# Float16 parts of q and k from the second pair of heads on, in an attention, Fourier and FFN kernel on one core

## The chip, the cores and the metric

The kernel runs on one core of a Trainium2 chip. The metric is the device time of one execution in microseconds. The kernel before took 1229.35 us, the median of three runs (1228.66 to 1231.81).

The engines are named as the profile names them: PE is TensorE, PEld its weight load, DVE is VectorE, ACT is ScalarE, POOL is GpSimd, SP is SyncE, which only issues DMAs.

## The reference

```python
def _attn_ref(q, k, v):                      # q, k, v: (8, 8, 576, 64) float32
    scores = scale * np.matmul(q, k.transpose(0, 1, 3, 2))
    scores = np.where(block_i >= block_j, scores, -1000000000.0)   # blocks of 64
    scores = scores - np.max(scores, axis=-1, keepdims=True)
    attn = np.exp(scores)
    attn = attn / (np.sum(attn, axis=-1, keepdims=True) + 1e-09)
    return np.matmul(attn, v)

def _moe_ref(x, w_ch1, w_ch2):               # x: (8, 576, 512), heads joined
    X = np.fft.fft(np.fft.fft(x, axis=1), axis=2)
    u = x + np.real(X)
    un = (u - mean(u)) / np.sqrt(var(u) + 1e-06)
    return u + np.maximum(un @ w_ch1, 0.0) @ w_ch2      # 512 -> 2048 -> 512
```

## The kernel before, in words

There are 8 batches of 8 heads. For each batch the kernel computes attention head by head, writes the result x to a DRAM tile (`xd`), reads it back straight and mirrored by rows, does a two-stage real Fourier transform by matmuls, normalizes, and sends the result through the two FFN matrices. All the matmuls work at close to float32 precision: an operand is split into a high and a low float16 part (or a float32r tile is used), and the products of the parts are summed in PSUM.

**A head.** `lead` and `rest` tiles hold q and k of a head side by side. `max_part` (L576) multiplies the high parts of q and k in four groups of matmuls, DVE reduces each to the row maxima `M`; `shift` (L605) transposes `M` on PE, ACT writes it as the row `mt`, and a DMA of 1.2 KB puts that row into the `lead` tile, so that the scores come out shifted. `scores` (L635) is four pieces: matmuls of `rest` and `lead`, then ACT makes the exponential twice (`ph` in float16, `p` in float32) and POOL subtracts them to the low part `pl`. `values` (L663) multiplies `ph` and `pl` by the parts of v (`VH`, `VL`) into `av`; after the last chunk DVE divides (`DEN`, `rec`, and `x` or `zc`), and after each second head two DMAs write to `xd`.

**How q and k get there.** Heads 0 to 7, the first batch, go by float32: `load_head` (L367) loads one head (64 rows of 1152 values, 295 KB), `lead` (L420) copies it on ACT into the tile of type float32r, `rest` (L430) takes the remainder of q on DVE and of k on POOL, and `lead_copies` puts two DMAs of 147 KB beside it. From head 8 on, pairs of heads go by float16: `load_pair` (L373) loads 128 rows (590 KB), `sum_qk` (L379) squares q and k on ACT for their sums, `scale` (L460) adds the sums over the partitions with one matmul and makes a power of two on DVE, `high` writes the scaled float16 parts on ACT, `low` the differences on DVE, and `high_copies` (L403) and `low_copies` (L413) bring each head's parts by two and two DMAs from the pair's tiles into the head's (147 KB and 295 KB). Three tiles `lead` and `rest` (`NB = 3`) are shared in turn by the heads.

**The weights.** Meanwhile the FFN's weights are loaded in 18 pieces by ACT's queue, brought from 64-bit integers' words to single precision by DVE (`W<-W`, three operations for a piece), and split: `weight_high` on ACT and `weight_parts` on PE and ACT for the first matrix.

**What sets the order.** All of this is written as lanes of `Step` objects. A planner in the same function keeps a clock of its own and books each step's chain on the engines' queues (D is DVE, A is ACT, G or P is POOL, Q is SP, M the DMA engines); `ready` (L298) says when a step may start, `issue` (L314) books and emits it, and the loop at L1248 chooses the next step by readiness and by `place`, a number near the head's. Steps with a cost use PE; steps of cost 0 ("free" steps) only use other engines and DMAs. The FFN's steps are the filler: one is issued whenever no step of a lane is ready. Each engine then runs its instructions in the order in which they were emitted. While the filler has not begun, all seven PSUM banks are lent to the other steps (`lent`).

**The transform.** `mirror` (L749) loads the first 256 rows (`u`) and 33 more (`X`) of `xd` on SP's queue, and gathers the mirrored rows by three indirect DMAs on POOL's. `folded` (L769) adds or subtracts straight and mirrored rows on DVE, in the order chunk 2 (33 rows), 0, 1.

Of the kernel before, what the change touches and what calls it, by code (L numbers as in the profile page):

```python
# [22 lines left out]
P = 128  # L23
# [8 lines left out]


HOP = 0.25
MARGIN = 0.3
AHEAD = (3.0, 6.0)
FREE = 0.5

# [163 lines left out]
def tile_attn_fourier_ffn(  # L202
# [47 lines left out]
    LEAD = [work.tile([P, 64 + 2 * S], F32R, name=f"lead{i}", bufs=1) for i in range(NB)]  # L250
    REST = [work.tile([P, 2 * S], F32R, name=f"rest{i}", bufs=1) for i in range(NB)]
    X1, X0, QA, QB = [], [], [], []

    def half_tiles():

        for i in range(NB):
            a = work.tile([P, 64 + 2 * S], F32, name=f"lead{i}", bufs=1).bitcast(F16)
            b = work.tile([P, 2 * S], F32, name=f"rest{i}", bufs=1).bitcast(F16)
            X1.append(a[0:KS, 0:64 + 2 * S])
            QA.append(a[:, 64 + 2 * S:64 + 4 * S])  # L260
            X0.append(b[:, 0:2 * S])
            QB.append(b[:, 2 * S:])
# [6 lines left out]
    for i in range(NB):  # L269
        gpsimd.dma_start(LEAD[i][D:KS], c_masks)  # L270
        vector.tensor_scalar(LEAD[i][0:D, 0:64], ones[0:D, 0:64], 0.0, None, op0=ALU.mult)
# [26 lines left out]
    def ready(step):  # L298
        r = max((done[x] for x in step.after), default=0.0)
        return max(r, min(rings[x][0] for x in lent)) if step.bank else r  # L300

    def book(engine, t, cost):

        used = [queues[x] for x in {"X": "DK", "G": "GK", "P": "G"}.get(engine, engine)]
        while True:
            at = max(x.fit(t, cost) for x in used)
            if at <= t:
                return max(x.book(t, cost) for x in used)
            t = at
# [63 lines left out]
    def load_pair(g):  # L373

        raws["pair", g] = work.tile([P, 2 * S], F32, name="raw", bufs=2)
        sync.dma_start(raws["pair", g], qk[2 * g:2 * g + 2].rearrange("h d s -> (h d) s"))
        yield

    def sum_qk(g):  # L379
        if not X1:  # L380
            half_tiles()
        raw, acc = raws["pair", g], sums(g)
        scalar.activation(QA[g % 2][:, 0:S], raw[:, 0:S], AF.Square, accum_out=acc[:, 1:2])
        yield
        scalar.activation(QB[g % 2][:, S:], raw[:, S:], AF.Square, accum_out=acc[:, 2:3])
        yield

    def high(g):
        raw, sc = raws["pair", g], scales[g]
        scalar.activation(QA[g % 2][:, 0:S], raw[:, 0:S], AF.Copy, scale=sc[:, 1:2])  # L390
        yield
        scalar.activation(QB[g % 2][:, S:], raw[:, S:], AF.Copy, scale=sc[:, 2:3])
        yield

    def low(g):
        raw, sc = raws.pop(("pair", g)), scales[g]
        a, b = QA[g % 2], QB[g % 2]
        vector.scalar_tensor_tensor(b[:, 0:S], raw[:, 0:S], sc[:, 1:2], a[:, 0:S], op0=ALU.mult, op1=ALU.subtract)
        yield
        vector.scalar_tensor_tensor(a[:, S:], raw[:, S:], sc[:, 2:3], b[:, S:], op0=ALU.mult, op1=ALU.subtract)  # L400
        yield

    def high_copies(h):  # L403
        x, at = X1[h % NB], slice(D * (h % 2), D * (h % 2 + 1))
        if h < H + NB:
            sync.dma_start(x[D:KS], c_masks16)
            vector.memset(x[0:D, 0:64], 0.0)
        g = h // 2
        sync.dma_start(x[0:D, 64:64 + S], QA[g % 2][at, 0:S])
        sync.dma_start(x[0:D, 64 + S:], QB[g % 2][at, S:])  # L410
        yield

    def low_copies(h):  # L413
        x, at = X0[h % NB], slice(D * (h % 2), D * (h % 2 + 1))
        g = h // 2
        sync.dma_start(x[0:D], QB[g % 2][at])
        sync.dma_start(x[D:P], QA[g % 2][at])
        yield
# [41 lines left out]
    def scale(g):  # L460

        acc = vsums.pop(g)
        t = ps_tile()
        mm(t[:, 0:3], ones, acc[:, 0:3], start=True, stop=True)
# [3 lines left out]
        vector.tensor_copy(n2, t[:, 0:3])  # L468
# [4 lines left out]
        for i in (1, 2):  # L473
# [3 lines left out]
        vector.tensor_scalar(  # L477
            x[:, 0:1], bits[:, 0:1], 0x7F000000, 1, op0=ALU.bitwise_and, op1=ALU.logical_shift_right
        )
        vector.tensor_scalar(to[:, 0:1], x[:, 0:1], -1, (190 + 14) << 23, op0=ALU.mult, op1=ALU.add)  # L480
# [14 lines left out]
    def split_v(g):  # L495

        acc = vsums.pop(g)
# [4 lines left out]
        sc = acc[:, 2:3]  # L502
        x = work.tile([P, 1], I32, name="pw", bufs=2)
        vector.tensor_copy(acc[:, 1:2], t[:, 0:1])
        vector.tensor_scalar(
            x, acc[:, 1:2].bitcast(I32), 0x7F000000, 1, op0=ALU.bitwise_and, op1=ALU.logical_shift_right
# [10 lines left out]
    def head_lane():  # L517
        for h in range(H):
            yield Step(
                lambda: load_head(h), 0.0, ("Q0.6", "M1.0", "L2.0"), (("T2", h - 2, 0), ("T2", h - 2, 1)) if h > 1 else (), ("L", h), place=h - 2.2  # L520
            )

        for g in range(H // 2, B * H // 2):
            done_with = (("T2", g + 2, 0), ("T2", g + 2, 1)) if g < H // 2 + 2 else (("lo", g - 2),)
            yield Step(lambda: load_pair(g), 0.0, ("Q0.6", "M2.2", "L2.0"), done_with, ("L", g), place=2 * g - 3.4)

    def pair_lane():
        for g in range(H // 2, B * H // 2):
            yield Step(
                lambda: sum_qk(g), 0.0, ("A0.86", "A0.86"), (("L", g),), ("QS", g), place=2 * g - 1.8,  # L530
# [818 lines left out]
```

## Time and profile before

| | us |
|---|---|
| median of three runs | 1229.35 |
| the profiled execution | 1229.43 |
| its span, first to last instruction | 1227.2 |
| PE busy in the span | 1146.5 (93%) |
| DVE busy | 693.3 (56%) |
| ACT busy | 564.2 (46%) |
| POOL busy | 423.2 (34%) |

Busy time is what an engine spends executing; waiting, branching and DMA-issuing are not in it. The granted clock (PEclk) is the share of PE's full clock that the chip let through. The chain of waits goes back from the last instruction to whatever released it, step by step, so a DMA stands in it with the time from its issue to the instruction that used it. Instructions of nearly all engines are recorded by one helper line (L195; L217 for matmuls), so groups are told apart by the names of the tiles that they write and read.

### The profile page before, as it was taken

The numbers are of one execution on the slowest core, as the hardware profiler recorded it, in microseconds if no ns is written. First come the engines' busy times: TensorE is split into PE (matmuls) and PEld (weight loads), VectorE is DVE, ScalarE is ACT, GpSimd is POOL, SyncE is SP. The second block draws the span as 40 slices with busy tenths as digits, with TensorE's granted clock in tenths as the row PEclk, the third lists the DMA queues.
The fourth block names the chain that finished last, engine by engine and source line by source line (L and its number), as shares of the span: only waits on it lengthen the run. The fifth ranks groups of instructions, "written<-read, shape, count | busy, mean of one in ns | idle before, by whom it ended". The sixth has DMA issues, their size and how long they took to land.

```text
span 1227.2 us, 25303 instructions
## 1 busy us (share of the span) xinstructions
PE 1146.5 (93%) x10116; PEld 823.7 (67%) x10116; DVE 693.3 (56%) x1514; ACT 564.2 (46%) x1257; POOL 423.2 (34%) x514
## 2 busy tenths in 40 slices
PE   5766878999899999999999999999999999999998
PEld 4663556576677777677777777776777667666665
DVE  6876777657747674766557555766474325431211
ACT  5565749655455445545465455644543112111110
POOL 4652525444333434354242633462425101200000
PEclk9566989999899999999999999999999999999999
DMA  7685344433224232421453224414230110000000
GB/s 208 176 296 177 108 129 113 113 109 87 73 71 126 74 87 70 135 65 47 117 150 82 80 65 130 108 38 124 60 96 15 37 37 6 18 18 1 18 18 18
DMA packets 65099, 107.38 MB, mean 87 GB/s; under 512 B 9504, under 2 KB 35304, under 8 KB 64982
## 3 DMA queue, kind: packets, MB, share of 16 engines
q1 hardware_dynamic: 57606, 81.37, 23.9%
q10 hardware_dynamic: 4384, 16.78, 4.1%
q0 software_dynamic: 2992, 7.62, 2.4%
q8 instruction: 79, 1.29, 0.5%
q14 instruction: 38, 0.31, 0.1%
HBM read 58.54 MB, written 18.89 MB: 63 GB/s over the span
## 4 chain that ended last, share of the span: by engine, by line
PE 82%; DVE 8%; DMA 3%; POOL 3%; ACT 2%; issue 1%; DVEq 0%; POOLq 0%; ACTq 0%; SPq 0%
PE h L217 30%; PE acc L217 30%; PE ps L217 15%; PE av L217 6%; DVE W L195 2%; DVE M L195 2%; PE ps L220 1%; DMA lead<-mt 1%; POOL pl L195 1%; DMA lead<-rest 1%; POOL u L195 1%; POOL ag L195 1%; DVE tmp L195 0%; DMA lead<-in_c_masks_dram 0%; DMA V<-in_v_dram 0%
## 5 line engine op out<-in xcount | busy, mean ns | idle before, releaser
L217 PE MATMUL h<-uh,W 128*128 128x256 f16 x2304 | 427.9, 273 | 1.2 <-DVE zc L195 1.2
L195 POOL TENSOR_TENSOR pl<-p,ph 128x288 f16<-128x288 f32 (+1 forms) x256 | 259.0, 1024 | 387.8 <-ACT p L195 365.5
L217 PEld LDWEIGHTS <-W 128*128 128x128 f16 x3456 | 332.1, 98 | 62.7 <-issue 2.3
L217 PE MATMUL acc<-W,gh 128*128 128x512 f16 x1104 | 329.6, 380 | 0.0
L217 PE MATMUL h<-ul,W 128*128 128x256 f16 x1152 | 314.4, 273 | 0.0
L195 DVE SCALAR_TENSOR_TENSOR gl<-h,gh 128x512 f16<-128x512 f32 x138 | 94.7, 688 | 208.5 <-ACT gh L195 208.4
L217 PE MATMUL acc<-W,gl 128*128 128x512 f16 x552 | 209.7, 380 | 1.3 <-DVE gl L195 1.3
L195 ACT ACTIVATE gh<-h 128x512 f16<-128x512 f32 x138 | 82.4, 597 | 275.8 <-PE h L217 275.7
L195 DVE TENSOR_REDUCE M<-ps 128x1 fp32r<-128x320 f32 (+3 forms) x293 | 130.9, 482 | 119.4 <-PE ps L217 119.1
L217 PE MATMUL ps<-lead 73*128 73x288 f16 (+13 forms) x702 | 160.8, 292 | 14.6 <-DMA lead<-in_c_masks_dram 7.0
L195 ACT ACTIVATE ph<-ps 128x512 f16<-128x512 f32 (+1 forms) x234 | 118.5, 507 | 111.6 <-PE ps L217 111.0
L217 PEld LDWEIGHTS <-gh 128*128 128x128 f16 x1104 | 102.7, 99 | 84.0 <-issue 3.2
L217 PEld LDWEIGHTS <-ph 128*128 128x128 f16 x1920 | 110.5, 102 | 26.6 <-DVE x L195 3.3
L195 ACT ACTIVATE p<-ps 128x512 f32<-128x512 f32 (+1 forms) x234 | 118.6, 509 | 1.9 <-POOL W L195 0.8
L217 PE MATMUL av<-VH,pl 128*128 128x65 f16 x960 | 113.6, 199 | 5.6 <-POOL pl L195 4.0
L217 PE MATMUL av<-VH,ph 128*128 128x65 f16 x960 | 114.5, 200 | 3.2 <-DVE x L195 1.7
L217 PE MATMUL av<-VL,ph 128*128 128x64 f16 x960 | 113.9, 198 | 0.0
L217 PEld LDWEIGHTS <-gl 128*128 128x128 f16 x552 | 53.8, 97 | 68.4 <-DVE gl L195 3.4
L217 PE MATMUL ps<-rest 128*128 128x320 f16 (+2 forms) x350 | 97.1, 291 | 2.8 <-DVE M L195 2.3
L217 PEld LDWEIGHTS <-pl 128*128 128x128 f16 x960 | 92.5, 101 | 7.0 <-POOL pl L195 5.4
L217 PEld LDWEIGHTS <-lead 73*128 73x128 f16 (+1 forms) x672 | 58.3, 100 | 33.8 <-issue 7.2
L217 PEld LDWEIGHTS <-rest 128*128 128x128 f16 x336 | 33.4, 100 | 22.5 <-issue 3.1
(202 smaller groups left out, 1415.0 us busy)
## 6 DMA issues: line engine op xcount, KB each, us to landing
raw<-in_qk_dram SPq DMA_DIRECT2D x28, 576.0 KB
W<-in_moe_w_ch_dram ACTq DMA_DIRECT2D x14, 1024.0 KB
rest<-lead SPq DMA_DIRECT2D x72, 144.0 KB
V<-in_v_dram SPq DMA_DIRECT2D x32, 320.0 KB
out_dram<-u SPq DMA_DIRECT2D x32, 256.0 KB
rest<-rest SPq DMA_DIRECT2D x56, 144.0 KB
xd<-x SPq DMA_DIRECT2D x30, 256.0 KB
u<-xd SPq DMA_DIRECT2D x8, 512.0 KB
```

Source lines behind the costliest of these rows:

```text
L195: x = f(*args, **kw)
L217: return tc.keep_in_program_order(nc.tensor.matmul(*args, **kw))
L220: return tc.keep_in_program_order(nc.tensor.transpose(*args, **kw))
```

## The change

Only heads 0 and 1 (`HF = 2`) still go by float32. The pair lane now starts at pair 1 (`GF = 1`), so heads 2 to 7 are loaded in pairs, squared, scaled, split and copied as the later batches are. Pair 1 has no tiles free yet: it is loaded as two halves into `zs0` and `zs1` and split into two stage tiles (`stage`, named u), and a weight load into one of those now waits for its copies. For pairs 1 to 3 `scale` makes q's and k's scale alone (`lo = 1`), and the scale of v stays in `split_v`.

Beside that: the 33-row load and the 33-row gather come first in `mirror`; the small tiles for the weights' split are a tile of their own (`turns`) and no longer a buffer of `x`; a free step of a place past 8 is ready only when the engine that it uses first would be open within 3 us of its own time (`BACKLOG`); the planner's hop is 0.3 in place of 0.25; the folds of batch 1 and the first feed's steps carry waits that the planner did not have; and when the filler begins, the planner's clock is set to where the lent PSUM banks are free.

```diff
+HF = 2
+GF = HF // 2
-HOP = 0.25
+HOP = 0.3
+BACKLOG = 3.0
...
     def ready(step):
         r = max((done[x] for x in step.after), default=0.0)
-        return max(r, min(rings[x][0] for x in lent)) if step.bank else r
+        if step.bank:
+            return max(r, min(rings[x][0] for x in lent))
+        if step.place > H and not step.cost:
+            for engine, cost in step.chain:
+                if engine in "DAGXP":
+                    return max(r, opening(engine, max(r, now), cost) - BACKLOG)
+                if engine not in scratch:
+                    break
+        return r
...
     def load_pair(g):
-        raws["pair", g] = work.tile([P, 2 * S], F32, name="raw", bufs=2)
-        sync.dma_start(raws["pair", g], qk[2 * g:2 * g + 2].rearrange("h d s -> (h d) s"))
+        given = qk[2 * g:2 * g + 2].rearrange("h d s -> (h d) s")
+        if g == GF:
+            raws["pair", g] = [work.tile([P, 2 * NSIN], F32, name=f"zs{i}", bufs=1) for i in range(2)]
+            for i in range(2):
+                sync.dma_start(raws["pair", g][i], given[:, S * i:S * (i + 1)])
+        else:
+            t = work.tile([P, 2 * S], F32, name="raw", bufs=2)
+            raws["pair", g] = t[:, 0:S], t[:, S:]
+            sync.dma_start(t, given)
         yield
...
     def pair_lane():
-        for g in range(H // 2, B * H // 2):
+        for g in range(GF, B * H // 2):
             yield Step(
-                lambda: sum_qk(g), 0.0, ("A0.86", "A0.86"), (("L", g),), ("QS", g), place=2 * g - 1.8,
-                need=((("TC", 2 * g - 3),) if g > H // 2 + 1 else (("S", H - 1, 2),)) + (("V", 2 * g - 5, 4),),
+                lambda: sum_qk(g), 0.0, ("A0.86", "A0.86"),
+                (("LP", g),) + ((("TC", 2 * g - 3),) if g > GF + 2 else ()) + ((("V", 2 * g - 5, 4),) if g > 2 else ()),
+                ("QS", g), place=2 * g - 1.8, need=(("S", g % 2, 2),) if GF < g < GF + 3 else (),
             )
+            if g < H // 2:
+                yield Step(lambda: scale(g, 1), 0.11, ("D0.2", "B", "D0.6"), (("QS", g),), ("SC", g), True, place=2 * g - 1.4)
...
     def copy_lane():
-        for h in range(H, B * H):
+        for h in range(HF, B * H):
...
     def prepare_lane():
-        for h in range(H):
+        for h in range(HF):
...
+            sync.dma_start(X[2], xd[256:289])
             sync.dma_start(LL, xd[0:256].rearrange("(c p) d -> p c d", p=P))
-            sync.dma_start(X[2], xd[256:289])
-            for dst, i in ((U[0], 0), (U[1], 1), (U2[0:33], 2)):
+            for dst, i in ((U2[0:33], 2), (U[0], 0), (U[1], 1)):
...
-                both = work.tile([P, 10 * D], F32, name="x", bufs=1)
+                both = work.tile([P, P + P // 2], F32, name="turns", bufs=1)
...
         if i is None:
-            lent = ["ps"]
+            if len(lent) > 1:
+                now = max(now, ready(filler), *rings["h"], *rings["acc"])
+                lent = ["ps"]
```

How the order moves, at three places. First SP's queue at the very start; `lead_84`/`rest_87` belong to head 0, `lead_85`/`rest_88` to head 1, `raw` is a load of q and k. Before:

```order
L195 DMA raw<-in_qk_dram 64x1152
L195 DMA rest_87<-lead_84 64x576 x2
L195 DMA raw<-in_qk_dram 64x1152
L195 DMA rest_88<-lead_85 64x576 x2
L195 DMA lead_84<-mt 1x5x128
L195 DMA V<-in_v_dram 128x640
```

With the change (`zs_124` and `zs_125` take pair 1, `lead_216` and `rest_217` are head 2's, copied from the stage tiles u):

```order
L200 DMA raw<-in_qk_dram 64x1152
L200 DMA zs_124<-in_qk_dram 128x576
L200 DMA zs_125<-in_qk_dram 128x576
L200 DMA rest_86<-lead_84 64x576 x2
L200 DMA raw<-in_qk_dram 128x1152
L200 DMA rest_87<-lead_85 64x576 x2
L200 DMA lead_84<-mt 1x5x128
L200 DMA V<-in_v_dram 128x640
L200 DMA raw<-in_qk_dram 128x1152
L200 DMA lead_85<-mt 1x5x128
L200 DMA lead_216<-in_c_masks_dram 9x1216
L200 DMA lead_216<-u 64x576 x2
```

Two loads of a whole pair now stand in front of head 0's row `mt`, and the copies of heads 2 and 3 follow it.

Second, DVE around the last output of the first batch's last head (`zc<-av,rec`); `VL` is the low part of v of the pair after, `rest`/`lead` with `vacc` the low parts of that pair's q and k. Before, from that output on:

```order
L195 TENSOR_TENSOR zc_1080<-av,rec 128x5x64
L195 COPY vacc<-acc 128x3
L195 TENSOR_SCALAR pw<-vacc 128x2
L195 SCALAR_TENSOR_TENSOR vacc<-pw 128x1 x2
L195 TENSOR_SCALAR pw<-vacc 128x1
L195 TENSOR_SCALAR vacc<-pw 128x1
L195 TENSOR_SCALAR x<-ident,wst 128x128
L195 CAST x<-ident 128x128
L195 TENSOR_SCALAR W<-W 128x1024
L195 SCALAR_TENSOR_TENSOR W<-W 128x1024
L195 MEMSET lead_1159 64x32
L195 SCALAR_TENSOR_TENSOR VL_96<-V,vacc,VH_94 128x640
```

With the change:

```order
L200 TENSOR_SCALAR pw<-vacc 128x1
L200 TENSOR_SCALAR vacc<-pw 128x1
L200 SCALAR_TENSOR_TENSOR VL_94<-V,vacc,VH_92 128x640
L200 TENSOR_SCALAR turns<-ident,wst 128x128
L200 CAST turns<-ident 128x128
L200 TENSOR_SCALAR DEN_91<-av,vacc 128x5
L200 RECIPROCAL rec<-DEN_91 128x5
L200 TENSOR_TENSOR zc_1131<-av,rec 128x5x64
L200 SCALAR_TENSOR_TENSOR rest_260<-raw,vacc,lead_259 128x576
L200 SCALAR_TENSOR_TENSOR lead_259<-raw,vacc,rest_260 128x576
L200 TENSOR_SCALAR W<-W 128x1024
L200 SCALAR_TENSOR_TENSOR W<-W 128x1024 x2
```

The scales, the low part of v and the small tiles for the weights moved from behind that output to in front of it.

Third, PE around the shift of head 9 (`ident,M`), with the sums of the next pair (`vacc,ones`) in front of it; `h<-uh,W` and `h<-ul,W` are the first feed. Before:

```order
L217 MATMUL av<-VL_96,ph_1564 128x64
L217 LDWEIGHTS pl_1565
L217 MATMUL av<-VH_94,pl_1565 128x65
L217 MATMUL ps<-vacc,ones 128x3
L217 MATMUL h<-ident,M_91 5x128
L217 LDWEIGHTS W
L217 MATMUL h<-uh,W 128x256
```

With the change, the end of 24 matmuls of the first feed that come after the sums:

```order
L222 MATMUL h<-uh,W 128x256
L222 LDWEIGHTS W
L222 MATMUL h<-ul,W 128x256
L222 LDWEIGHTS W
L222 MATMUL h<-uh,W 128x256
L222 MATMUL ps<-ident,M_89 5x128
```

Eight steps of the first feed moved from behind head 9's shift to in front of it.

## Rows read from the trace of the kernel before

**Rows 1.** The page: span, and busy us (share) of each engine.

```profile
span 1227.2 us, 25303 instructions
PE 1146.5 (93%) x10116; PEld 823.7 (67%) x10116; DVE 693.3 (56%) x1514; ACT 564.2 (46%) x1257; POOL 423.2 (34%) x514
```

**Rows 2.** Stretches: start:end, length, busy (x count) by engine, PEclk, DMA share, GB/s.

```profile
0.00:8.00 8.00, 1.00 (x4) 1.03 (x5) 2.18 (x17) 3.27 (x4) 4.14 (x9) 1.00 0.78 165
8.00:20.00 12.00, 4.09 (x14) 2.88 (x13) 10.57 (x22) 3.87 (x7) 1.85 (x3) 1.00 1.03 282
20.00:36.00 16.00, 14.31 (x136) 12.65 (x136) 12.22 (x22) 11.60 (x25) 12.97 (x12) 0.99 0.45 124
36.00:60.00 24.00, 17.02 (x132) 14.89 (x133) 19.47 (x38) 14.44 (x33) 14.11 (x15) 0.50 0.68 202
60.00:96.00 36.00, 24.56 (x240) 21.86 (x240) 24.79 (x48) 23.03 (x50) 21.79 (x24) 0.59 0.85 277
96.00:150.00 54.00, 41.72 (x151) 22.66 (x151) 40.14 (x74) 34.33 (x69) 18.73 (x29) 0.77 0.45 145
...
340.00:1227.00 887.00, 877.24 (x7822) 627.67 (x7819) 450.19 (x1004) 358.42 (x812) 268.69 (x335) 1.00 0.24 66
```

**Rows 3.** PE's waits, 36 to 96 us: us in total, times, longest us.

```profile
PE ps L217 <- DVE M L195: 3.9, 2, 2.6
PE acc L217 <- DMA lead<-mt: 3.3, 1, 3.3
...
PE av L217 <- POOL pl L195: 2.2, 4, 1.0
PE acc L217 <- ACT lead L195: 1.9, 1, 1.9
```

**Rows 4.** The chain of waits, 0 to 160 us: start us, us, what.

```profile
11.83 8.46 DMA lead<-mt
...
43.70 5.67 DMA lead<-mt
...
102.45 5.99 DMA lead<-rest
```

**Rows 5.** ACT's groups, 0 to 96 us: busy us, mean ns, idle before and releaser.

```profile
L195 ACT CAST lead<-raw 64x1152 fp32r<-64x1152 f32 x8 | 9.2, 1144 | 7.1 <-DMA raw<-in_qk_dram 7.1
...
L195 ACT ACTIVATE lead<-raw 128x576 f16<-128x576 f32 x1 | 0.7, 741 | 0.0
...
L195 ACT ACTIVATION_READ_ACCUMULATOR lead<-raw 128x1 f32 x1 | 0.3, 261 | 0.0
```

**Rows 6.** Groups of DVE, then of POOL, 0 to 96 us.

```profile
L195 DVE TENSOR_TENSOR rest<-raw,lead 64x576 fp32r<-64x576 f32 x8 | 7.6, 951 | 1.0 <-ACT lead L195 1.0
...
L195 POOL TENSOR_TENSOR rest<-raw,lead 64x576 fp32r<-64x576 f32 x8 | 14.1, 1766 | 5.7 <-ACT lead L195 5.3
```

**Rows 7.** DVE's timeline, 96 to 115 us: start us, us, instruction [idle before].

```profile
96.39 0.49 DVE L195 TENSOR_TENSOR zc<-av,rec 128x320 f32<-128x320 f32 x1
...
103.19 0.88 DVE L195 SCALAR_TENSOR_TENSOR VL<-V,vacc,VH 128x640 f16<-128x640 f32 x1 [3.24 <-ACT VH L195]
...
105.12 0.81 DVE L195 SCALAR_TENSOR_TENSOR rest<-raw,vacc,lead 128x576 f16<-128x576 f32 x1
...
108.95 0.56 DVE L195 TENSOR_REDUCE M<-ps 128x2 fp32r<-128x128 f32 x2 [2.28 <-PE ps L217]
...
110.53 2.48 DVE L195 SCALAR_TENSOR_TENSOR W<-W 128x1024 int32<-128x1024 int32 x2
...
114.31 0.67 DVE L195 TENSOR_TENSOR tmp<-X,U 33x512 f32<-33x512 f32 x1
```

**Rows 8.** PE's waits, 150 to 200 us.

```profile
PE h L217 <- DVE M L195: 7.6, 1, 7.6
```

**Rows 9.** PE's timeline, from 160 us.

```profile
162.21 0.44 PE L217 MATMUL h<-uh,W 128*128 128x256 f16 x1
162.44 0.42 PE L217 MATMUL h<-ul,W 128*128 128x256 f16 x1
```

More of the change, by code (lines that the diff above doesn't have):

```diff
@@ L249, in tile_attn_fourier_ffn, with half_tiles, both, split @@
     NB = 3
[L250 to L262, printed above, removed]
+    LEAD = [work.tile([P, 64 + 2 * S], F32R, name=f"lead{i}", bufs=1) for i in range(HF)]
+    REST = [work.tile([P, 2 * S], F32R, name=f"rest{i}", bufs=1) for i in range(HF)]
+    halved = {}
+    def half_tiles(i):
+        if i not in halved:
+            a = work.tile([P, (64 + 2 * S) // (1 if i < HF else 2)], F32, name=f"lead{i}", bufs=1).bitcast(F16)
+            b = work.tile([P, 2 * S // (1 if i < HF else 2)], F32, name=f"rest{i}", bufs=1).bitcast(F16)
+            halved[i] = (a[0:KS, 0:64 + 2 * S], b[:, 0:2 * S]) + ((a[:, 64 + 2 * S:64 + 4 * S], b[:, 2 * S:]) if i < HF else ())
+        return halved[i]
+    def both(h):
+        return half_tiles(h % NB)[0:2]
+    def split(g):
+        if g == GF:
+            return tuple(stage[i].rearrange("p c d -> p (c d)").bitcast(F16)[:, 0:2 * S] for i in range(2))
+        return half_tiles(g % 2)[2:4]
     M = [const.tile([P, 6], F32R, name=f"M_{i}") for i in range(2)]
@@ L299, in ready, with shared, opening @@
         r = max((done[x] for x in step.after), default=0.0)
[L300 to L309 removed]
+        if step.bank:
[7 more added lines that the diff above has]
+        return r
+    def shared(engine):
+        return [queues[x] for x in {"X": "DK", "G": "GK", "P": "G"}.get(engine, engine)]
+    def opening(engine, t, cost):
+        while True:
+            at = max(x.fit(t, cost) for x in shared(engine))
+            if at <= t:
+                return t
+            t = at
+    def book(engine, t, cost):
+        t = opening(engine, t, cost)
+        return max(x.book(t, cost) for x in shared(engine))
     pending = []
@@ L377, in load_pair @@
         yield
     def sum_qk(g):
[L380 to L383, printed above, removed]
+        (rq, rk), acc = raws["pair", g], sums(g)
+        a, b = split(g)
+        scalar.activation(a[:, 0:S], rq, AF.Square, accum_out=acc[:, 1:2])
         yield
-        scalar.activation(QB[g % 2][:, S:], raw[:, S:], AF.Square, accum_out=acc[:, 2:3])
+        scalar.activation(b[:, S:], rk, AF.Square, accum_out=acc[:, 2:3])
```

93 lines of the change are left out of this document (48 added, 45 removed).

## The prediction

> **What bounds the kernel now.** The page comes first: TensorE (PE) is busy 1146.5 of 1227.2 us [rows 1]. The table of stretches says how much is lost where [rows 2]. From 340 us to the end PE is busy 877.24 of 887 us at full clock: nothing that moves work about inside that stretch can gain more than 9.8 us, and the change takes no matmul of the FFN or the transform away. So the time is decided before 340 us. There PE sits idle 35 us in the first 96 us (the eight heads of the first batch), and 12.3 us from 96 to 150 (weights are split and the first transform runs); the 190 us after that hold most of the rest. Once PE is saturated, a microsecond by which this start gets shorter is a microsecond of the end.
>
> What holds PE in the first stage is read from its waits between 36 and 96 us [rows 3]. Their list sums to 18.4 us: 6.7 us on the maxima that VectorE (DVE) reduces (three rows, the first is shown), 4.2 us on the small row of shifts (mt, 1.2 KB by DMA; two rows, the longer is shown), 2.2 us on the parts pl that GpSimd (POOL) makes, 1.9 us on ScalarE's (ACT) copy of a head's q and k, the rest singly. DVE is the fullest engine there: 19.47 of 24 and 24.79 of 36 us [rows 2]. The chain of waits shows what the DMA queues do to it: the row mt took 8.46 and 5.67 us from issue to its use, and a float16 head's copies 5.99 us [rows 4]. From 8 to 20 us the 16 DMA engines are full at 282 GB/s; from 20 to 36 us they are less than half used [rows 2].
>
> **The change part by part.**
>
> *The start, heads 0 and 1.* These stay as they were, but the loads of the second and third pair now stand on SP's queue in front of the first row mt: 590 KB for pair 1 and 590 KB in the place of one head's 295 KB, 885 KB more. Lower bound nothing: in the first 8 us the engines moved 165 GB/s, so at 282 GB/s another 0.94 MB had room there. Upper bound: all of it behind full engines, 885 KB at 202 GB/s, the rate from 36 to 60 us, 4.4 us. At 282 GB/s it is 3.1 us. The squares of pair 1 also stand ahead of mt on ACT (two of 0.74 us with an accumulator read of 0.26 us [rows 5]), in time that ACT idles. I take **+2 us** (0 to +4.4), nearest the 282 GB/s row with a part hidden in the first 8 us.
>
> *Heads 2 to 7.* Removed per head: ACT's copy of 1.144 us, DVE's rest of 0.951 us, POOL's rest of 1.766 us [rows 5, 6]. Added per pair: on ACT two squares with reads and two scaled copies, 2 x (0.74 + 0.26) + 2 x 0.74, 3.5 us against 2.3; on DVE two products with a difference of 0.81 us [rows 7] and four tiny operations (0.15 us each, an estimate: a third of the 0.49 us row of [rows 7]), 2.2 us against 1.9. Over three pairs ACT gains 3.6 us of work, DVE 0.9, POOL loses 10.6. ACT is busy 37.5 of the 60 us from 36 to 96 [rows 2], so its extra lies beside other work. POOL's relief reaches PE only through pl, at most 2.2 us [rows 3]. What is late now is different: the load. ACT waited 7.1 us for raw loads [rows 5], and PE 1.9 us for that copy. With whole pairs loaded early those go. PE also gets more between a head's last maxima and its shift: in the order the shift of head 4 now follows the scores of head 3 and the last values of head 2, and that of head 6 the scores of head 5, where before only one group of values stood between. I take half of the 6.7 us on maxima, the 1.9 us, 1 us of pl and 1 us of mt: 3.3 + 1.9 + 1 + 1, **-7 us**. Bounds: 0, if DVE alone sets the pace, and -18.4, if all waits went.
>
> The new cost here is a hop. A float16 head can start its maxima only after two copies have landed; before, ACT wrote the tile itself. The nearest row is the copies' 5.99 us, and in the worst case a slow mt of 8.46 us [rows 4]. I cost it at nothing because the order issues the copies one to two heads ahead of their maxima, and a head took about 12 us (96 us for 8). If the copies come less than a hop ahead, each head pays up to 6 us; that is the second rival.
> [...]
>
> *From the last head to the first feed.* In the trace DVE ends the last head's output at 96.9 us and starts the first fold at 114.3 us [rows 7], 17.4 us. In it stand a wait of 3.24 us for ACT (parts of v, queued behind the parts of pair 4) and one of 2.28 us for maxima whose tile came by copies. The change has pair 4's squares, scales and high parts before the last head's values, so both waits, 5.5 us, lose their cause. What is left on DVE there: pair 4's low parts, 2 x 0.81 us; one weight piece of 2.48 us and a shorter operation, some 3.2 us; and the maxima with a second piece, which took from 108.95 to 114.31, 5.4 us [rows 7]. That is 10.2 us and gaps, so 11 to 13 in the place of 17.4. The 33-row load and gather, now first on SP's and on POOL's queue, belong to the fold that comes first in the order; where DVE is the later one, as here, this is worth nothing, and it costs the load of u one small issue. Against it, the scales and v's low part now lie before the last head's output, 0.88 us and six tiny operations, 1.8 us of DVE. I take **-4 us** (-6 to 0).
>
> *After it.* The longest wait of PE after the first stage is 7.6 us in front of head 9's shift [rows 8]. The order now has eight steps, 24 matmuls of the first feed, between; they start 0.22 us apart there [rows 9], so 5.3 us at half clock, 2.6 at full clock. But head 15's and head 21's shifts lose most of what stood ahead of them. **-2 us** net (-7.6 to +3). Rules that only move later work (free steps of heads past 8 held back while their engine is booked over 3 us ahead, the hop of 0.3, the waits added for the first feed and the second batch's folds) fall where PE is nearly full: **0** (-3 to +5); their cover is the queue of feed matmuls, and a step held back too long would show as a wait of PE for maxima or scales.
>
> Sum: 2 - 7 - 4 - 2 = -11 us. The profiled execution itself took 1229.43 us (span 1227.2), the median of the three runs is 1229.35, so either gives **1218.4 us**.
>
> **The rivals.**
>
> *DVE keeps the pace.* DVE is busy 69 of the first 96 us (2.18 + 10.57 + 12.22 + 19.47 + 24.79) [rows 2] and the change gives it 0.9 us more. If its queue rather than loads orders the heads, the 7 us are not there: 1229.4 + 2 + 0.9 - 4 - 2 = 1226.3. For it: the waits on maxima are the largest sum of PE's waits [rows 3]. Against: DVE is at 72%, not full.
>
> *The DMA queue turns it slower.* Each float16 head has 442 KB of copies where a fp32 head had 295 KB, on the same queue as the rows mt. If from head 2 on these transfers take what the slow mt rows took, 5.67 us, and half of that has no cover in four of the six heads, that is 11.3 us; with the full 4.4 us at the start: 1229.4 + 4.4 + 11.3 - 4 - 2 = 1239.1. It decides when the mt rows of more than three of heads 2 to 7 take over 5 us. For it: 0.85 of the DMA time is already used from 60 to 96 us. Against: from 20 to 60 us there is room [rows 2].
> By the Trainium skill, DMA: Bandwidth & Descriptors, section on queues, rings and completion order, each issuing queue is one ring per DMA engine and is consumed in ring order; the 8.46 us of a 1.2 KB row bears that out.
>
> *The clock stays up.* From 36 to 96 us PE was granted 0.50 to 0.59 of its clock [rows 2], near the lower of its two levels (1.2 of 2.4 GHz). From 96 to 150 us it was 0.77 with PE busy 41.72 us, so 9.6 us of that is the lower level. If denser heads keep the clock up until the weights are split and PE sets the pace there: 1218.4 - 9.6 = 1208.8. Against: PE is still idle a quarter of the time before.
>
> *The gain is given back.* A new wait of PE past 200 us (head 15, head 21) with a fall of the clock after it eats it: about 1229.
>
> **How the numbers follow.** The forecast gets 0.52, the clock 0.13, DVE's pace 0.15, the gain given back 0.05, the DMA queue 0.15. The range takes in the clock's case, with the lower bounds of the other terms below it, and reaches most of the way to the slower rival's: 1204 to 1237; the forecast's own is 1211 to 1225. About 0.3%, 3.7 us, is what a measurement of this kernel can tell from no change, so the bounds are 1225.7 and 1233. Faster: 0.52 + 0.13 + 0.05 of DVE's case, 0.70. Same: the other 0.10 and 0.05, 0.15. Slower: 0.15.
>
> **What would show it.** Right: the last values of the first batch end near 92 us (96.9 now), the first fold starts about 13 us after, PE is saturated some 11 us earlier, no raw-load wait is left on ACT, and PE's busy time stays near 1146 us less what the clock saves. Wrong: the first mt later than 25 us, the first batch's end at 96 us or after it, or over 10 us of PE's idle time past 340 us.

## The result and the profile after

| us | before | after |
|---|---|---|
| median, four runs each | 1230.58 (1228.66 to 1233.05) | 1213.66 (1211.96 to 1216.37) |
| profiled execution | 1229.43 | 1216.37 |
| its span | 1227.2 | 1214.6 |

The ratio is 0.9861 [0.9832, 0.9891], 17 us less, where 11 were forecast. The profiled executions are 13.1 us apart: that of after is the slowest of its four. Its page, to be held against [rows 1], with the tenths of the granted clock (its first slices are not to be read as they stand, see below):

```profile
span 1214.6 us, 25361 instructions
PE 1145.7 (94%) x10122; PEld 818.8 (67%) x10122; DVE 691.0 (57%) x1525; ACT 568.6 (47%) x1269; POOL 417.0 (34%) x507
...
PEclk9998899999799999999999999999999999999999
```

PE's work stayed (0.8 us less busy time), and its idle time fell from 80.7 to 68.9 us: the gain is idle time of PE. The stretches, as in [rows 2]:

```profile
0.00:8.00 8.00, 1.25 (x5) 1.28 (x6) 2.37 (x17) 3.17 (x5) 3.63 (x8) 1.00 0.75 180
8.00:20.00 12.00, 4.41 (x15) 3.13 (x14) 11.20 (x28) 6.37 (x12) 1.90 (x3) 1.00 1.04 327
20.00:36.00 16.00, 14.64 (x116) 12.61 (x117) 11.38 (x20) 10.71 (x26) 10.25 (x9) 1.00 0.72 210
36.00:60.00 24.00, 18.36 (x159) 12.61 (x157) 21.20 (x50) 17.43 (x40) 11.98 (x16) 1.00 0.84 258
60.00:96.00 36.00, 24.81 (x240) 17.45 (x240) 27.03 (x58) 22.31 (x51) 18.87 (x20) 0.98 0.79 249
96.00:150.00 54.00, 40.35 (x198) 23.56 (x196) 43.95 (x69) 36.63 (x76) 23.16 (x34) 0.85 0.45 136
```

The extra loads show at 8 to 20 us: 327 GB/s where 282 were moved before. DVE is fuller from 36 to 96 us (48.2 of 60 us with 108 instructions; before 44.3 with 86). The column of the granted clock reads 1.00 and 0.98 from 36 to 96 us, 0.50 and 0.59 before. But this trace holds no record of the clock before 91.1 us (the one of the kernel before begins at 28.9 us), and a time without a record counts as 1.00 in the column. What PE's pace was there is read from its matmuls, in the last section.

PE's waits, 36 to 96 us, against [rows 3]:

```profile
PE acc L222 <- DMA lead<-mt: 6.5, 4, 2.5
PE av L222 <- POOL pl L200: 5.6, 8, 1.3
...
PE ps L222 <- DVE M L200: 1.1, 2, 0.7
```

The wait for maxima went from 6.7 to 1.1 us, but the rows mt rose from 4.2 to 6.5 and the parts pl from 2.2 to 5.6. All the waits listed there sum to 16.5 us, 18.4 before: mostly one kind took the place of another. ACT's raw loads in the first 96 us (groups of ACT, as in [rows 5]) are left for heads 0 and 1 alone:

```profile
L200 ACT CAST lead<-raw 64x1152 fp32r<-64x1152 f32 x2 | 2.3, 1152 | 4.1 <-DMA raw<-in_qk_dram 4.1
```

The chain of waits, against [rows 4]; its rows run from a DMA's issue to the use of what it brought:

```profile
12.24 8.10 DMA lead<-mt
32.45 5.18 DMA lead<-mt
41.84 5.12 DMA lead<-mt
...
61.37 6.10 DMA lead<-mt
```

DVE's timeline around the last head's output (zc) and the first fold (tmp<-X,U), against [rows 7]:

```profile
93.58 0.88 DVE L200 SCALAR_TENSOR_TENSOR VL<-V,vacc,VH 128x640 f16<-128x640 f32 x1 [4.52 <-ACT VH L200]
...
95.18 0.49 DVE L200 TENSOR_TENSOR zc<-av,rec 128x320 f32<-128x320 f32 x1
95.59 0.81 DVE L200 SCALAR_TENSOR_TENSOR rest<-raw,vacc,lead 128x576 f16<-128x576 f32 x1
...
97.77 2.48 DVE L200 SCALAR_TENSOR_TENSOR W<-W 128x1024 int32<-128x1024 int32 x2
100.17 0.55 DVE L200 TENSOR_REDUCE M<-h 128x2 fp32r<-128x128 f32 x2
...
103.12 2.48 DVE L200 SCALAR_TENSOR_TENSOR W<-W 128x1024 int32<-128x1024 int32 x2
105.53 0.68 DVE L200 TENSOR_TENSOR tmp<-X,U 33x512 f32<-33x512 f32 x1
```

From the end of zc to the fold it is 9.9 us, 17.4 before, without a wait between. The wait for ACT's VH is not gone: it stands in front of zc now, 4.52 us long. It ended at 93.58 us, and the last values that zc needs ended at 93.5, so nearly all of it lay beside the wait for those. Last, PE's waits from 150 to 200 us, against [rows 8]:

```profile
PE h L222 <- ACT tmp L200: 2.9, 1, 2.9
PE ps L222 <- DVE M L200: 2.8, 3, 2.2
```

The 7.6 us in front of head 9's shift are gone.

**The same steps in every kernel.** This table is read from the profiled execution of each kernel below: the end of the last values of heads 0 and 7 on PE, the start of the first fold on DVE, the end of the second transpose of the first feed on PE (t1), the ends of the first and second of 18 feeds, and the end of the last.

| us | head 0 | head 7 | fold | t1 | feed 1 | feed 2 | last feed |
|---|---|---|---|---|---|---|---|
| before | 29.9 | 95.9 | 114.3 | 150.3 | 236.9 | 301.0 | 1223.0 |
| after | 30.2 | 93.5 | 105.5 | 143.5 | 228.8 | 290.7 | 1210.5 |
| e1_gather | 27.7 | 93.7 | 109.8 | 145.5 | 237.4 | 301.5 | 1224.1 |
| e2_planner | 28.9 | 95.0 | 109.8 | 150.0 | 235.9 | 298.2 | 1240.0 |
| e3_half_only | 29.6 | 94.6 | 103.4 | 145.0 | 228.6 | 298.1 | 1227.2 |
| e4_mt_pool | 28.6 | 94.7 | 106.4 | 144.2 | 230.8 | 292.7 | 1211.9 |
| e5_no_stt | 30.1 | 89.2 | 99.8 | 134.9 | 221.7 | 283.6 | 1203.0 |
| e6_pair4_late | 29.3 | 91.8 | 107.0 | 141.9 | 228.8 | 290.7 | 1210.0 |
| e7_load2_late | 29.2 | 92.0 | 104.2 | 142.3 | 227.8 | 289.7 | 1208.7 |
| e8_before_mt_pool | 29.2 | 96.5 | 114.5 | 150.3 | 242.5 | 306.6 | 1228.5 |
| e9_hop | 29.4 | 98.9 | 107.9 | 150.1 | 239.2 | 296.8 | 1235.9 |
| e10_no_backlog | 29.6 | 93.5 | 105.2 | 142.8 | 233.0 | 304.6 | 1230.0 |
| e11_no_lent | 29.3 | 92.6 | 104.3 | 142.6 | 230.5 | 292.3 | 1215.9 |
| e12_old_gather | 29.4 | 93.6 | 105.6 | 143.1 | 231.6 | 293.4 | 1212.7 |

Between the ends of two feeds lie heads and feeds in an order of each plan's own, so that single columns there can differ by what was moved; the last one counts.

So the 12.5 us between the two profiles came as 2.4 by head 7, 4.4 more by t1, 5.7 more after it.

How far a single execution strays is seen where the order is the same. The order of e1_gather is that of the kernel before until head 7 has ended, and yet its heads 0 and 7 end 2.2 us earlier. The order of e10_no_backlog, e11_no_lent and e12_old_gather is that of the changed kernel as far; they end head 0 at 29.3 to 29.6 us, the changed kernel at 30.2. So one or two microseconds at a single step show nothing. The way from head 0 to head 7 holds: 66.0 and 66.0 us in the first order, 63.3 to 64.2 in the second. So does the way from t1 to the last feed: 1072.7 to 1078.6 us in the three kernels with PE's order of before (before, e1_gather, e8_before_mt_pool), 1066.4 to 1069.6 in the four whole kernels with PE's order of the change (after, e4_mt_pool, e7_load2_late, e12_old_gather).

### The profile page after: what moved, and what is told of

The parts are those of the page before. It is cut to its first block, busy times and chain, and to the rows that moved or that the text cites. A ratio compares the mean times of both kernels' runs of the same rounds, so it can differ in the third digit from the quotient of the medians.

```text
span 1214.6 us, 25361 instructions
## 1 busy us (share of the span) xinstructions
PE 1145.7 (94%) x10122; PEld 818.8 (67%) x10122; DVE 691.0 (57%) x1525; ACT 568.6 (47%) x1269; POOL 417.0 (34%) x507
## 4 chain that ended last, share of the span: by engine, by line
PE 83%; DVE 6%; DMA 5%; POOL 2%; ACT 2%; issue 2%; SPq 0%; DVEq 0%; ACTq 0%; POOLq 0%
PE acc L222 30%; PE h L222 30%; PE ps L222 15%; PE av L222 6%; DMA lead<-mt 2%; DVE W L200 2%; PE ps L225 1%; DVE M L200 1%; DMA lead<-rest 1%; POOL u L200 1%; DMA u<-in_moe_w_ch_dram 1%; POOL pl L200 1%; DMA V<-in_v_dram 0%; ACT p L200 0%; SPq L200 0%
## 5 line engine op out<-in xcount | busy, mean ns | idle before, releaser
L222 PE MATMUL h<-uh,W 128*128 128x256 f16 x2304 | 433.0, 274 | 0.0
L222 PE MATMUL ps<-lead 73*128 73x288 f16 (+7 forms) x708 | 162.8, 293 | 16.7 <-DMA lead<-in_c_masks_dram 6.7
L200 ACT ACTIVATE ph<-ps 128x288 f16<-128x288 f32 (+1 forms) x235 | 119.0, 508 | 99.1 <-PE ps L222 98.2
L222 PEld LDWEIGHTS <-ph 128*128 128x128 f16 x1920 | 114.2, 103 | 24.5 <-issue 5.1
L200 ACT ACTIVATE p<-ps 128x288 f32<-128x288 f32 (+1 forms) x235 | 118.0, 505 | 2.1 <-POOL pl L200 1.0
L222 PE MATMUL av<-VH,ph 128*128 128x65 f16 x960 | 117.0, 202 | 0.7 <-ACT p L200 0.7
L222 PE MATMUL ps<-rest 128*128 128x320 f16 (+3 forms) x356 | 98.3, 291 | 1.6 <-DVE M L200 1.3
L222 PEld LDWEIGHTS <-lead 73*128 73x128 f16 (+1 forms) x744 | 66.1, 103 | 39.0 <-issue 6.5
L222 PEld LDWEIGHTS <-rest 128*128 128x128 f16 x372 | 38.7, 104 | 30.6 <-issue 11.8
```

The lines of the kernel that those rows point to most:

```text
L200: x = f(*args, **kw)
L222: return tc.keep_in_program_order(nc.tensor.matmul(*args, **kw))
```

## The experiments

Each ratio is to the kernel before, run beside the experiment on the same chip.

### One part of the change alone, on the kernel before

**Gather and load of the 33 rows first.**

```diff
+            sync.dma_start(X[2], xd[256:289])
             sync.dma_start(LL, xd[0:256].rearrange("(c p) d -> p c d", p=P))
-            sync.dma_start(X[2], xd[256:289])
-            for dst, i in ((U[0], 0), (U[1], 1), (U2[0:33], 2)):
+            for dst, i in ((U2[0:33], 2), (U[0], 0), (U[1], 1)):
```

> The kernel before with the 33-row load and gather first, nothing else. My theory (DVE reaches the folds after the gathers have landed, so their order is free): within 1 us of the kernel before, 1229.5 to 1231. Rival (the gathers set the start of the transform): the first fold starts 2 to 5 us sooner after the last output of the first batch than the 17.4 us of before, and the time is 1225 to 1228.

Measured: 1230.3, ratio 0.9998 [0.9982, 1.0014]. t1 is 4.8 us earlier than before, but 2.2 of these are there when head 7 ends, ahead of what was edited. From head 7 to the fold it takes 16.1 us, before 18.4: 2.3 us are the gather's, and the rival's sign in the trace is there. Feed 1 ends no earlier (237.4). From t1 to there PE runs the same instructions in the same order and is busy 78.0 us, before 69.9, while it idles less (13.9 and 16.7): it worked at a lower clock. From 180 to 200 us it was granted 0.75, before 1.00:

```profile
180.00:200.00 20.00, 17.66 (x132) 12.62 (x130) 16.24 (x39) 16.56 (x37) 6.77 (x6) 0.75 0.39 105
```

e8_before_mt_pool, whose t1 is as late as before's, takes the same long way from t1 to feed 1 (92.2 us; before 86.6). So that loss does not come of an earlier t1, and the profile cannot tell what became of the 2.3 us. The time does not show them.

**The planner's rules alone** (hop 0.3, BACKLOG, the added waits, the clock set when the filler begins).

```diff
-HOP = 0.25
+HOP = 0.3
+BACKLOG = 3.0
...
+                lent = ["ps"]
```

> The kernel before with the planner's new rules alone (hop 0.3, free steps held back, waits of the first feed and of the second batch's folds, the clock set at the first feed); heads 2 to 7 stay float32. My theory (most of the 17 us come from the first 150 us and so from the float16 path): 1226 to 1233. Rival (the rules avoid waits after 150 us and give half of the gain or more): 1222 or less.

Measured: 1247.1, ratio 1.0128 [1.0105, 1.0151]: 16 us slower. The rules do not suit the old path. Its stretch from 96 to 150 us:

```profile
96.00:150.00 54.00, 32.02 (x123) 19.32 (x124) 42.47 (x77) 28.20 (x55) 20.34 (x28) 0.72 0.54 163
```

PE idles 22.0 of 54 us there, 12.3 in the kernel before, and what it waits for (96 to 165 us) is a head's copies and, more in sum, the weights' split:

```profile
PE h L218 <- DMA lead<-rest: 8.2, 1, 8.2
PE ps L218 <- DVE wst L196: 5.4, 1, 5.4
PE ps L218 <- ACT W L196: 4.7, 3, 3.4
```

The steps of the table do not show this at once: t1, feed 1 and feed 2 end no later than before's. The work that PE did not do in that time comes later, and the last feed is 17.0 us late. Over the whole execution PE idles 10.0 us more and is busy 7.0 us more.

**The float16 path with the old rules** (the gather, `turns` and the two added waits kept).

```diff
-HOP = 0.3
+HOP = 0.25
...
-        if step.place > H and not step.cost:
...
-                now = max(now, ready(filler), *rings["h"], *rings["acc"])
```

> The changed kernel with the planner's old rules (hop 0.25, no holding back of free steps, no setting of its clock at the first feed); the float16 path and the early gather stay. My theory: 1213 to 1219, most of the gain is left. Rival (the rules give half or more): 1222 or more.

Measured: 1236.98, ratio 1.0033 [1.0012, 1.0055]. Up to the end of feed 1 it is as good as the whole change (228.6 and 228.8). Then it falls back: 7 us by feed 2, another 9 by the end. Head 9's stall stays, in PE's waits from 150 to 200 us:

```profile
PE ps L222 <- DVE M L200: 9.4, 3, 7.6
```

This kernel comes nearest to the rival "the gain is given back": under the old rules the new path loses all that it saved. (Its profile is of one of its quicker executions, 1233.13 us.)

### One part taken out of the changed kernel

**Without holding back free steps.**

```diff
-        if step.place > H and not step.cost:
-            for engine, cost in step.chain:
...
```

> The changed kernel without the holding back of free steps; hop 0.3 and the rest kept. If that rule keeps the gain (theory: without it DVE and ACT get steps of later heads and pairs in front of the ones that PE waits for), this run is at 1225 or more, and the loss lies after the first feed. Rival (the hop does it): 1212 to 1219.

Measured: 1237.02, ratio 1.0056 [1.0039, 1.0074]. PE's order is that of the change until head 9; t1 is 142.8. Then PE's waits from 150 to 200 us:

```profile
PE ps L222 <- DVE DEN L200: 7.7, 1, 7.7
PE ps L222 <- DVE M L200: 3.5, 1, 3.5
```

The 7.7 us are in front of head 9's shift again. Feed 2 ends 13.9 us later than after's, the last feed 19.5.

**The hop of 0.25.**

```diff
-HOP = 0.3
+HOP = 0.25
```

> The changed kernel with the planner's hop back at 0.25, its other new rules kept. So far: old rules together put the changed kernel at 1237, the new ones at 1214, with the same time up to the first feed's end (228.6 and 228.8 us) in both traces. If the hop is the rule that keeps the gain (theory: it makes the planner put more feed matmuls in front of each wait for maxima, shifts and scales), this run is at 1225 or more. Rival (holding back free steps does it): 1212 to 1219.

Measured: 1238.79, ratio 1.006 [1.004, 1.0079]. Here the order differs from the start, and the first batch is where it begins to lose: head 7 ends at 98.9. Head 9's shift has its wait again too, 6.32 us. PE's waits, 36 to 96 us:

```profile
PE h L222 <- DMA lead<-mt: 6.0, 1, 6.0
PE ps L222 <- DVE M L200: 4.3, 2, 3.5
PE av L222 <- DVE dft L200: 3.7, 1, 3.7
```

**Without the clock set when the filler begins.**

```diff
-            if len(lent) > 1:
-                now = max(now, ready(filler), *rings["h"], *rings["acc"])
-                lent = ["ps"]
+            lent = ["ps"]
```

> The changed kernel without the setting of the planner's clock when the first feed takes its PSUM banks back. Theory (a booking rule for one moment at 150 us): the same as the changed kernel within 3 us, 1211 to 1217. Rival (the first feed is then planned too early and PE waits in front of it): 1219 or more, with the loss before 200 us.

Measured: 1221.3, ratio 0.9921 [0.9895, 0.9947], just clear of the changed kernel's interval, and in the rival's range. But e12_old_gather, which keeps the changed order on PE and ran beside it on the same chip, is at 1218.99 with an interval that overlaps. In the profiles e11_no_lent is 1.6 us behind by feed 2 and 5.4 at the end, while PE idles no more over the whole execution (68.0 us, after 68.9) and is busy 6.2 us more. A loss through waits, as the rival has it, is not shown.

**The load and gather in the old order.**

```diff
+            sync.dma_start(LL, xd[0:256].rearrange("(c p) d -> p c d", p=P))
             sync.dma_start(X[2], xd[256:289])
-            sync.dma_start(LL, xd[0:256].rearrange("(c p) d -> p c d", p=P))
-            for dst, i in ((U2[0:33], 2), (U[0], 0), (U[1], 1)):
+            for dst, i in ((U[0], 0), (U[1], 1), (U2[0:33], 2)):
```

> The changed kernel with the loads and gathers of the mirrored rows in the old order (33 rows last), every other instruction in its place. In the kernel before, the early gather shortened the stretch from the first batch's last values to the first feed's transposes from 54.4 to 51.8 us without a gain in the whole. Theory now (with pair 4's copies done early, the gather of the 33 rows is what the first fold waits for): 2 to 4 us slower than the changed kernel, 1216 to 1218, the first fold later by as much. My theory of the prediction (DVE is the later one, the order of the gathers is free): 1212 to 1215.

Measured: 1218.99, ratio 0.9904 [0.9877, 0.9931], which overlaps the changed kernel's. The first fold on DVE:

```profile
105.63 0.68 DVE L200 TENSOR_TENSOR tmp<-X,U 33x512 f32<-33x512 f32 x1 [0.23 <-DMA U<-xd,rows]
```

It waits 0.23 us for the gather and starts 0.1 us later than in the changed kernel, so here the gather's place does not set the fold. The 5 us between the medians of this kernel and the changed one are not its doing by this trace, and the intervals overlap.

**Pair 4's squares held back until head 7's scores are done.** This takes away the cause that I had given for the shorter way from the last head to the fold.

```diff
-... need=(("S", g % 2, 2),) if GF < g < GF + 3 else (),
+... need=(("S", g % 2, 2),) if GF < g < GF + 3 else (("S", H - 1, 2),) if g == H // 2 else (),
```

> The changed kernel with the squares of pair 4 (the second batch's first) held until the first batch's last scores, as they were before. My theory (the 4 us between the first batch's last output and the first feed come from pair 4's work done earlier): the wait for ACT and for the copies come back behind the last output, the first fold starts about 17 us after it, and the time is 1216 to 1219. Rival (that stretch is set by the weights' splitting on PE and ACT): 1212 to 1215.

Measured: 1217.74, ratio 0.9907 [0.9882, 0.9932]. The median lies where I expected it. In the trace a part of the old way comes back:

```profile
92.27 0.49 DVE L200 TENSOR_TENSOR zc<-av,rec 128x320 f32<-128x320 f32 x1
...
98.23 0.89 DVE L200 SCALAR_TENSOR_TENSOR VL<-V,vacc,VH 128x640 f16<-128x640 f32 x1 [2.49 <-ACT VH L200]
...
106.99 0.68 DVE L200 TENSOR_TENSOR tmp<-X,U 33x512 f32<-33x512 f32 x1
```

The wait for VH stands behind the last output again, and from the end of zc to the fold it is 14.2 us (9.9 in the changed kernel, 17.4 before). But the last output itself is 2.9 us earlier, so that the fold starts 1.5 later, and t1 is 1.6 earlier. So the fold does not set t1. What the rival names, the weights' split, is PE's largest wait from 96 to 150 us in the changed kernel:

```profile
PE ps L222 <- ACT W L200: 4.7, 5, 2.2
```

From the end of feed 1 on the two profiles run together, and the profiled execution is not slower than after's (1215.88 and 1216.37). What the early squares are worth in the whole is not shown: the 4 us in the medians have no place in the profile, and the intervals overlap.

### The disputed costs by themselves

**The rows mt of the first batch on GpSimd's queue, in the changed kernel.**

```diff
-            sync.dma_start(both(h)[0][KM:KS, 0:640].rearrange("r (j p) -> r j p", j=5), mt)
+            (gpsimd if h < H else sync).dma_start(both(h)[0][KM:KS, 0:640].rearrange("r (j p) -> r j p", j=5), mt)
...
-        sync.dma_start(dst.bitcast(F32), mt.bitcast(F32))
+        gpsimd.dma_start(dst.bitcast(F32), mt.bitcast(F32))
```

> The changed kernel with the first batch's rows mt issued on GpSimd's queue, with the order of all else the same. My theory (in the first 96 us PE waits 11.3 us for these rows because they stand behind the pair loads and copies on SP's queue): the waits of PE for mt fall below 4 us, the last values of the first batch end 3 to 8 us earlier, 1206 to 1211. Rival (the 16 DMA engines are full, so any queue waits; or DVE sets the pace): the waits for mt stay over 8 us or turn into others, 1212 to 1216.

Measured: 1216.96, ratio 0.9876 [0.984, 0.9911]. The chain of this kernel:

```profile
12.95 5.81 DMA lead<-mt
...
31.13 4.73 DMA lead<-mt
...
40.01 5.62 DMA lead<-mt
...
50.13 6.28 DMA lead<-mt
```

Head 0's row became quicker, 5.81 us for 8.10 (6.65 to 7.90 in other executions of the same order), and head 0 ends 1.6 us earlier. By the semaphores' times in the trace, which give the rows that the chain leaves out, so did head 1's (8.35 to 5.72) and head 6's (4.24 to 2.31), while head 4's became slower (2.83 to 6.28). PE's waits for mt (36 to 96 us) are no less than the 6.5 us of after:

```profile
PE acc L222 <- DMA lead<-mt: 7.8, 3, 3.6
PE av L222 <- POOL pl L200: 7.5, 8, 1.5
```

**The same in the kernel before**, whose first batch has the float32 form alone.

```diff
-        sync.dma_start(dst.bitcast(F32), mt.bitcast(F32))
+        gpsimd.dma_start(dst.bitcast(F32), mt.bitcast(F32))
```

> The kernel before with the first batch's rows mt on GpSimd's queue, all else in the same order. My theory (before, maxima on DVE and raw loads held the first batch as much as these rows): 1226 to 1230. Rival (the rows on SP's queue alone held it): 1224 or less.

Measured: 1232.35, ratio 0.9994 [0.9976, 1.0013]. The place in SP's queue is then not what makes a row of 1.2 KB slow, except perhaps for the first two; what the others wait for is not shown. Issuing from GpSimd did not slow every row: the quickest took 1.58 us from issue to landing here, and 1.78 us on SP's queue in the kernel before.
By the Trainium skill, DMA: Bandwidth & Descriptors, section on queues, rings and completion order, a DMA engine takes packets by turns from the rings that have work for it. I take from that that a row alone on another queue should hardly wait behind bulk copies: the 8.10 us that became 5.81 agree in direction, the rows of 4.73 to 6.28 us do not show it, and my reading of the 8.46 us [rows 4] as ring order holds for the first rows at most.

**The load of pair 2 issued behind head 0's row mt.**

```diff
+    late = []
...
+            if g == 2:
+                late.append((t, given))
+            else:
+                sync.dma_start(t, given)
...
+        if h == 0:
+            sync.dma_start(*late.pop())
```

> The changed kernel with the load of pair 2 issued behind head 0's row mt in place of in front of it, nothing else. My theory (885 KB more in front of that row cost the start about 2 us): the row lands 2 to 3 us earlier, the first head's values come 2 us earlier, and the time falls by 0 to 2 us, 1211 to 1214. Rival (pair 2 is then late and heads 4 and 5 wait for it): 1215 or more.

Measured: 1215.2, ratio 0.9868 [0.9832, 0.9904]. Head 0 ends 1.0 us earlier (29.2) and head 7 1.5, hardly more than the executions of one order differ by (29.3 to 30.2 and 92.6 to 93.6); the time is the same within the intervals.

**Two of DVE's three operations for a weight piece replaced by memsets of 16 columns.** DVE's queue is relieved of 2.48 us for a piece, and the kernel leaves the weights unfinished.

```diff
-        vector.scalar_tensor_tensor(t, r[:, 0], 29, t, op0=ALU.logical_shift_right, op1=ALU.bitwise_or)
+        vector.memset(t[:, 0:16], 0)
...
-        vector.scalar_tensor_tensor(t, r[:, 1], -(1 << 30), t, op0=ALU.bitwise_and, op1=ALU.bitwise_or)
+        vector.memset(t[:, 16:32], 0)
```

> The changed kernel with two of the three DVE operations that bring each weight piece to single precision replaced by tiny ones, in the same order: the weights are left wrong, so that DVE loses about 2.4 us a piece, some 19 us of its work in the first 96 us. If DVE sets the pace of the first batch, its last values end 8 us or more earlier than 93.5 us and the time falls below 1205. My theory (loads and small rows by DMA set it): the last values end less than 4 us earlier, and the time is 1207 to 1213, by shorter waits between 96 and 150 us.

Measured: 1207.83, ratio 0.9799 [0.9763, 0.9834]. Head 7 ends 4.3 us earlier than after's, between what I had put for the two theories; t1 is 8.6 us earlier, the last feed 7.5. Now the first fold waits for the gather:

```profile
99.80 0.68 DVE L200 TENSOR_TENSOR tmp<-X,U 33x512 f32<-33x512 f32 x1 [1.37 <-DMA U<-xd,rows]
```

So this work of DVE does hold the start, for 4 us in the first batch and as much again between it and the first feed; and 7.5 of the 8.6 us saved by t1 reach the end. In the second stretch it may be DVE's queue, or the weights' split, which now gets its pieces earlier; the run does not tell them apart. No kernel that does all the work beat the changed one.

## Why the prediction was right, and where it was not

The sign and the range held (1213.66 in 1204 to 1237). Against the profiled executions the sum was 11 for 12.5 us. That it came so near is luck in part. The terms were not all as I had them: heads 2 to 7 gave 4.3 us less than forecast, the stretch after t1 gave 3.7 us more, and the two errors nearly cancel.

| term | forecast | measured in the profiles |
|---|---|---|
| start, heads 0 and 1 (head 0's end) | +2 | +0.3 |
| heads 2 to 7 (head 0's end to head 7's) | -7 | -2.7 |
| last head to the first feed (head 7 to t1) | -4 | -4.4 |
| after it (t1 to the last feed) | -2 and 0 | -5.7 |

**The start** was rather priced too high, but the runs do not pin it down. The two loads ahead of the row mt found room: 327 GB/s instead of 282 from 8 to 20 us, and mt took 8.10 us as it had taken 8.46. But head 0 ends at 27.7 and 29.9 us in two executions of the old order and at 29.3 to 30.2 in four of the new, so the +0.3 stands for anything from below nothing to 2.5. The 1.0 us of e7_load2_late is no more than the executions of one order differ by.

**Heads 2 to 7** is the term that was mis-sized most: 2.7 us for 7 (1.8 to 2.7 over the executions of the same two orders). The raw-load waits of these heads went as I had said (4.1 of the 7.1 us stay, in front of heads 0 and 1), and of the 6.7 us on maxima more than the half that I took, 5.6 us. What I did not count is what is late next: I let the waits on mt and pl fall by 1 us each, and they rose by 2.3 and 3.4. So the list of waits lost 1.9 us in all. The rival "DVE keeps the pace" has a part in it: DVE is fuller by 4.0 us from 36 to 96 us, and taking its weight pieces away lets head 7 end 4.3 us earlier.

**From the last head to the fold** the size was right, and the fold came at 105.5, where my numbers give 105 (92 and 13). The two halves of that were off against each other: the last output ended at 95.7 instead of 92, and the way from it to the fold took 9.9 us instead of 11 to 13. Of the two waits that I had removed, that for maxima is gone, and that for VH (3.24 us) moved ahead of the output and grew to 4.52, but lies beside the wait for the last values there. Pair 4's early squares are a cause of the shorter way to the fold: held back, they bring 4.4 of the 7.5 us back between the last output and the fold. They are not shown to be a cause of an earlier t1, which they did not make later. That the gather's place is worth nothing in the changed kernel was right (0.23 us of wait). On the kernel before, where I had not asked, the gather alone brought the fold 2.3 us nearer to head 7's end, and nothing of it was seen at the end of feed 1.

**After the first feed** the step "rules that only move later work: 0" failed. It took the rules one by one as costs behind a cover, and never asked what the float16 path would do without them. With the old rules the way from t1 to the last feed is 1082.2 us, in the kernel before 1072.7, in the changed one 1067.0: there the rules are worth 15.2 us in the profiles, more than my whole forecast (by the ratios of the two kernels 1.7%, 21 us). Head 9's 7.6 us, which I put down to eight feed steps between, is the piece that can be followed: it comes back at 7.6 us without the rules, at 7.7 without BACKLOG alone and at 6.3 with the old hop alone. The other pieces are spread; PE's waits past 340 us sum to 2.9 us in the profile after, and to 11.5 and 11.9 in e10_no_backlog and e9_hop, over nine and seven kinds of wait.

The parts do not add. The path alone (with the gather, `turns` and the added waits) is 0.3% slower than before, the rules alone 1.3% slower, both together 1.4% faster; taking out BACKLOG or the hop alone costs 2%. How much of such a step belongs to the rule, and how much to the chance that another number puts the whole greedy order on another track, the runs do not tell: that would need several values of each number, and stays open.

**The rivals.** "The DMA queue turns it slower" came close to its sign in the trace: three of the rows mt of heads 2 to 7 took over 5 us (5.18, 5.12 and 6.10), where I had asked for more than three; the others took 2.83, 4.24 and 4.74. PE's wait for them was up by half. It did not decide: on another queue four rows were over 4.7 us as well, and the time no better.

"The clock stays up" is not settled for the first batch. The 1.00 and 0.98 from 36 to 96 us are no sign of it, since the trace has no record of the clock before 91.1 us. With the old gather (e12_old_gather) the order up to the gather is the same, and the record begins at 41.3 us:

```profile
60.00:96.00 36.00, 23.09 (x239) 16.74 (x240) 27.16 (x58) 22.22 (x51) 18.78 (x20) 0.59 0.79 251
```

Head 7 ends at 93.6 us there and at 93.5 in the changed kernel, and the values' matmuls have the same length (last section), so both ran at the lower level for most of that stretch. What the full clock would be worth to the first batch no run shows. From 96 to 150 us, for which my 9.6 us were worked out, it only rose from 0.77 to 0.85. Behind t1 the clock has a price: e1_gather and e8_before_mt_pool took 5.3 and 5.6 us longer than the kernel before to the end of feed 1, with PE's order the same and 8.1 us more of PE's busy time in each. Between the two kernels' own profiles it makes no difference there: both were granted 1.00 from 166 to 260 us.

## What to carry to other kernels

A new data path and the constants of the scheduler that orders it are one change: price the path with the old constants as a case of its own, since here it lost everything that way. Time saved ahead of the saturated stretch counts only as far as the order behind it stays covered; follow it at two or three fixed steps (here t1, feed 1, feed 2) instead of subtracting it from the end. Compare first two executions whose order is the same: what they differ by at a step (here two microseconds) is no finding. And where a wait goes, look for what is next in line in the same stage before booking it: five microseconds on maxima came back as six on two others.

## What was unexpected of the hardware

The column of the granted clock can read near 1 while PE runs at its lower level. The values' matmuls, PE, 60 to 96 us, at 0.98 in the changed kernel, where the record only begins at 91.1 us:

```profile
L222 PE MATMUL av<-VH,ph 128*128 128x65 f16 x60 | 10.4, 239 | 0.7 <-ACT p L200 0.7
```

At 0.59 with the old gather:

```profile
L222 PE MATMUL av<-VH,ph 128*128 128x65 f16 x60 | 10.3, 238 | 0.7 <-ACT p L200 0.7
```

And in the changed kernel from 200 to 220 us, at a recorded 1.00:

```profile
200.00:220.00 20.00, 18.35 (x170) 10.72 (x169) 13.38 (x30) 16.83 (x39) 13.82 (x13) 1.00 0.37 98
L222 PE MATMUL av<-VH,ph 128*128 128x65 f16 x25 | 2.9, 195 | 0.0
```

In the first two, matmuls of the values that follow one another mostly start 54 ns apart, in the last 29 ns. So the length of one and the same form, and how far apart its starts lie, tell the level where the column does not.

A row of 1.2 KB took 4.73 to 6.28 us on GpSimd's queue for heads 2 to 5, about what three of the rows took on SP's behind the bulk copies (5.12 to 6.10), so that a queue of its own bought no time.
